# Windowed attention and a channel mix on one core: new engine choices, new orders, keys of the sinks copied on three engines

## The chip, the cores and the metric

The kernel runs on one core of one Trainium2 chip. The metric is the device time of one execution in microseconds. The five engines of the core work side by side and each takes its instructions in the order in which they were written: TensorE (PE; its weight loads are listed as PEld), VectorE (DVE), ScalarE (ACT), GpSimd (POOL) and SyncE (SP), which here only starts DMAs. Engines wait for one another through semaphores.

## The reference

Four batches of eight heads with 768 positions of 64 numbers go through attention with a window of 128 positions and four positions at the start (the sinks) that every query sees. The result, 768 x 512 per batch, goes through a channel mix with gate.

```python
keep = is_sink | in_window              # pos < 4, or 0 <= query - key < 128
a = softmax(where(keep, q @ k.T / 8, -1e9))
x = concat_heads(a @ v)                 # (4, 768, 512)
xk = mu_k * x + (1 - mu_k) * x_prev     # x_prev: one position earlier, zeros first
xr = mu_r * x + (1 - mu_r) * x_prev
k = maximum(xk @ w_k, 0)                # 512 -> 1024
v = (k * k) @ w_v                       # 1024 -> 512
out = sigmoid(xr @ w_r) * v
```

## The kernel before

The work is cut into 12 units u of 256 positions, three to a batch (T = 0, 1, 2). For each unit there are these steps:

- Load q, k and v of all heads in float32 (L479 to L509, on SP), and cast them to bf16 in halves (L732 to L743 for q and k, L813 for v). Then q and k are turned: for units 0 to 4 (k) and 0 to 6 (q) by PE and a copy out of PSUM (L776, L781, L794, L799), later by a transposing DMA on SP (L758). The results are `kt` and `qt`.
- `attend`: scores by pairs of heads (L877) into the tiles `sc`, exponentials on ScalarE (`e`, L949), a mask multiplied in on VectorE (L963), products with v on PE (L982), and division by the sums on VectorE (`rec`, L996; `x`, L999). In units 1 and 2 (the list `BIAS`) the mask is added on PE ahead of the scores (L886). In T = 1 and 2 the four sinks are a product of their own: their keys are copied out of `kt` into `ksink` (L830), scored with q of one or two units (L846), go through the exponential (`es`) and are multiplied with the sinks' values (`vsink`; L935 by quarters of the array, L920 in full form).
- `mix`: x is turned (by PE up to unit 5, L1023 and L1032; from unit 6 on by a transposing DMA, L1043, on SP), then `td`, `xk` and `xr` are made on VectorE (L1059, L1072).
- `ffn`: hidden products (L1150), relu (`rl`, L1160 or L1164), square (`kk`, L1172), gate (L1181, `th`), output products (L1199), result (`ob`, L1208), store (L1215, on SP).

The weights w_k, w_r and w_v come in 1 MB pieces (L522) and are cast by L693 to L699. PE's matmuls on the tile `warm` (L1257 to L1263) only fill gaps up to 28.5 us.

Every operation is recorded as one step of a `Plan` with a number (in the order of recording), a cost, the buffers that it takes and holds, and the data that it reads and writes. Two tables of numbers then settle the program. `CHOICE` names the engine, or the form on PE, for operations that can go several ways. `ORDER` gives, for each engine, the numbers in the order of issue. `schedule` walks these five lines, by its costs, in order to interleave them, assign buffers and place the gap fillers; it does not reorder within an engine. `LOADS` gives ranks to the first loads; the order on SP is the table's.

Of the kernel before, what the change touches and what calls it, by code (L numbers as in the profile page):

```python
# [18 lines left out]
    81: "DVE", 83: "ACT", 88: "ACT", 89: "DVE", 90: "DVE", 91: "ACT", 92: "POOL",  # L19
    93: "ACT", 94: "ACT", 95: "DVE", 96: "ACT", 97: "DVE", 98: "ACT", 100: "DVE",  # L20
    101: "DVE", 103: "ACT", 104: "POOL", 106: "DVE", 107: "POOL", 109: "ACT", 110:
    "POOL", 111: "DVE", 135: "POOL", 137: "ACT", 138: "DVE", 140: "DVE", 141: "ACT",
    143: "ACT", 144: "ACT", 146: "ACT", 147: "ACT", 148: "DVE", 150: "DVE", 157:
    "DVE", 167: "PE/tiles", 178: "PE/tiles", 187: "POOL", 189: "ACT", 190: "ACT",
    192: "ACT", 193: "POOL", 195: "ACT", 196: "POOL", 198: "ACT", 199: "POOL", 200:
    "ACT", 202: "DVE", 209: "ACT", 217: "ACT", 221: "ACT", 225: "DVE", 229: "ACT",
    247: "PE/tiles", 258: "PE/tiles", 267: "POOL", 269: "ACT", 270: "POOL", 272:
    "ACT", 273: "POOL", 275: "DVE", 276: "ACT", 278: "ACT", 279: "ACT", 280: "DVE",
    283: "ACT", 290: "DVE", 298: "DVE", 302: "ACT", 306: "ACT", 310: "DVE", 346:
    "POOL", 348: "ACT", 349: "POOL", 351: "ACT", 352: "ACT", 354: "ACT", 355: "DVE",  # L30
    357: "ACT", 358: "ACT", 359: "POOL", 361: "DVE", 368: "ACT", 376: "ACT", 380:
    "ACT", 384: "ACT", 388: "ACT", 402: "DVE", 403: "POOL", 405: "ACT", 406: "POOL",
    408: "ACT", 410: "ACT", 411: "ACT", 412: "ACT", 416: "PE/tiles", 428:
    "PE/tiles", 440: "ACT", 447: "ACT", 455: "ACT", 459: "ACT", 463: "ACT", 467:
    "ACT", 482: "PE/tiles", 494: "PE/tiles", 505: "POOL", 506: "ACT", 508: "ACT",
    509: "POOL", 511: "POOL", 513: "ACT", 514: "POOL", 515: "ACT", 518: "ACT", 525:
    "ACT", 533: "ACT", 537: "ACT", 541: "ACT", 545: "ACT", 581: "POOL", 582: "POOL",
    583: "ACT", 585: "POOL", 587: "POOL", 588: "DVE", 603: "ACT", 607: "ACT", 611:
    "ACT", 615: "ACT", 629: "ACT", 630: "ACT", 631: "ACT", 633: "POOL", 635: "ACT",
    636: "POOL", 640: "PE/tiles", 652: "PE/tiles", 677: "ACT", 681: "ACT", 685:  # L40
    "ACT", 689: "ACT", 704: "PE/tiles", 716: "PE/tiles", 727: "POOL", 728: "POOL",
    729: "ACT", 731: "POOL", 733: "ACT", 734: "ACT", 750: "ACT", 754: "ACT", 758:
    "ACT", 762: "ACT", 798: "POOL", 799: "POOL", 800: "ACT", 802: "ACT", 804:
    "POOL", 805: "DVE", 820: "ACT", 824: "ACT", 828: "ACT", 832: "ACT", 846: "ACT",
    847: "POOL", 848: "ACT", 850: "POOL", 852: "ACT", 853: "POOL", 857: "PE/full",
    869: "PE/tiles", 894: "ACT", 898: "ACT", 902: "ACT", 906: "ACT", 921:
    "PE/tiles", 933: "PE/full", 958: "ACT", 962: "DVE", 966: "ACT", 970: "ACT", 986:
    "DVE", 990: "ACT", 994: "ACT", 998: "DVE",
# [336 lines left out]
def kernel(  # L385
# [14 lines left out]
    nc = tc.nc  # L400
# [4 lines left out]
    NS = 4  # L405
# [44 lines left out]
    def act(n):  # L450
        return 80.0 + 0.805 * n
# [869 lines left out]
```

## Time and profile before

| what | value |
|---|---|
| median of 3 runs | 163.8 us (163.5 to 166.03) |
| profiled execution, its own time | 165.17 us |
| its span | 163.5 us |
| granted TensorE clock | 1.0 |
| PE, VectorE, ScalarE, GpSimd busy | 155.4, 144.3, 115.4, 35.5 us |
| HBM read, written | 24.15, 6.29 MB |

Busy time counts an instruction from its start to its end. Matmuls overlap, so PE's busy time also holds the tail of each; an idle stretch of PE that the profile names is one in which no matmul was under way. The chain of work is followed back from the last instruction: at each step to what released it, or to the instruction before it on its engine.

### The profile page before, as it was taken

The numbers are of one execution on the slowest core, as the hardware profiler recorded it, in microseconds if no ns is written. First come the engines' busy times: TensorE is split into PE (matmuls) and PEld (weight loads), VectorE is DVE, ScalarE is ACT, GpSimd is POOL, SyncE is SP. The second block draws the span as 40 slices with busy tenths as digits, with TensorE's granted clock in tenths as the row PEclk, the third lists the DMA queues.
The fourth block names the chain that finished last, engine by engine and source line by source line (L and its number), as shares of the span: only waits on it lengthen the run. The fifth ranks groups of instructions, "written<-read, shape, count | busy, mean of one in ns | idle before, by whom it ended". The sixth has DMA issues, their size and how long they took to land.

```text
span 163.5 us, 4724 instructions
## 1 busy us (share of the span) xinstructions
PE 155.4 (95%) x1867; PEld 101.1 (62%) x1867; DVE 144.3 (88%) x378; ACT 115.4 (71%) x182; POOL 35.5 (22%) x71
## 2 busy tenths in 40 slices
PE   7888999899999999999998989999999999999992
PEld 3445557785487557677484548567466856574841
DVE  5268987999999999999999699999989999998852
ACT  3388989999979899899867856867269977042220
POOL 5943402250032152130232303030040110000000
PEclk9999999999999999999999999999999999999999
DMA  4888999999899999999999999899999973180133
GB/s 144 242 242 220 321 339 338 384 386 347 206 271 273 204 219 231 203 278 138 192 188 255 150 296 245 148 256 144 262 213 233 224 236 64 32 190 38 64 128 128
DMA packets 80361, 35.46 MB, mean 217 GB/s; under 512 B 69964, under 2 KB 72276, under 8 KB 80340
## 3 DMA queue, kind: packets, MB, share of 16 engines
q1 hardware_dynamic: 80180, 34.97, 97.2%
q8 instruction: 14, 0.23, 0.6%
q10 hardware_dynamic: 160, 0.20, 0.3%
q14 instruction: 7, 0.06, 0.1%
HBM read 24.15 MB, written 6.29 MB: 186 GB/s over the span
## 4 chain that ended last, share of the span: by engine, by line
PE 61%; DVE 14%; DMA 10%; SPq 9%; ACT 2%; issue 1%; DVEq 0%
PE bank L1199 20%; PE bank L1150 19%; PE bank L1181 10%; DMA w<-in_moe_w_k_dram 7%; PE bank L982 4%; SPq L496 4%; DVE e L963 3%; PE sc L877 3%; SPq L479 3%; DMA xt<-x 3%; DVE x L999 2%; DVE xr L1072 2%; DVE xk L1072 2%; PE bank L776 2%; DVE kk L1172 2%
## 5 line engine op out<-in xcount | busy, mean ns | idle before, releaser
L949 ACT ACTIVATE e<-sc 128x1024 bf16<-128x1024 f32 (+1 forms) x48 | 44.6, 958 | 6.2 <-PE sc L877 6.2
L1150 PE MATMUL bank<-xk,wk_sb 128*128 128x256 bf16 x384 | 47.0, 273 | 0.6 <-DVE wk_sb L699 0.6
L1199 PE MATMUL bank<-wv_h,kk 128*128 128x512 bf16 x184 | 44.0, 379 | 0.0
L1150 PEld LDWEIGHTS <-wk_sb 128*128 128x128 bf16 x384 | 36.3, 98 | 6.9 <-DVE wk_sb L699 0.8
L1160 ACT ACTIVATE rl<-bank 128x512 bf16<-128x512 f32 x42 | 24.7, 604 | 18.9 <-PE bank L1150 17.5
L1199 PEld LDWEIGHTS <-kk 128*128 128x128 bf16 x184 | 16.9, 98 | 17.8 <-issue 0.2
L963 DVE TENSOR_TENSOR e<-e,mask 128x1024 bf16<-128x1024 bf16 (+1 forms) x40 | 25.3, 652 | 0.4 <-ACT e L949 0.4
L1181 PE MATMUL bank<-wr_sb,xr 128*128 128x512 bf16 x96 | 23.7, 379 | 0.0
L1072 DVE SCALAR_TENSOR_TENSOR xk<-td,mu_all,xt 128x256 bf16<-128x256 bf16 x48 | 23.4, 517 | 0.0
L1072 DVE SCALAR_TENSOR_TENSOR xr<-td,mu_all,xt 128x256 bf16<-128x256 bf16 x48 | 22.3, 484 | 0.0
L1172 DVE TENSOR_TENSOR kk<-rl 128x512 bf16<-128x512 bf16 x48 | 19.9, 430 | 0.9 <-ACT rl L1160 0.8
L1187 ACT ACTIVATE th<-bank 128x512 f32<-128x512 f32 x24 | 13.8, 604 | 8.9 <-PE bank L1181 8.9
L999 DVE TENSOR_TENSOR x<-bank,rec 128x256 bf16<-128x256 f32 x48 | 19.3, 415 | 0.4
L1208 DVE SCALAR_TENSOR_TENSOR ob<-th,bank 128x512 f32<-128x512 f32 x23 | 15.3, 677 | 2.8 <-ACT th L1187 1.9
L982 PE MATMUL bank<-vb,e 128*128 128x65 bf16 x352 | 16.3, 194 | 0.2 <-DVE vb L813 0.2
L982 PEld LDWEIGHTS <-e 128*128 128x128 bf16 x352 | 13.7, 97 | 3.5 <-issue 0.3
L1181 PEld LDWEIGHTS <-xr 128*128 128x128 bf16 x96 | 8.9, 98 | 8.5
L813 POOL CAST vb<-vs 128x512 bf16<-128x512 f32 x8 | 6.8, 856 | 31.4 <-DMA vs<-in_v_dram 21.7
L877 PE MATMUL sc<-qt,kt 64*64 64x128 bf16 (+3 forms) x496 | 12.7, 226 | 0.1
L877 PEld LDWEIGHTS <-kt 64*64 64x64 bf16 (+1 forms) x496 | 8.9, 106 | 6.0 <-issue 4.9
L736 POOL CAST qb<-qs 128x512 bf16<-128x512 f32 x8 | 5.8, 720 | 27.7 <-issue 9.5
L1059 DVE TENSOR_TENSOR td<-xt 128x512 bf16<-128x512 bf16 x24 | 9.9, 419 | 1.5 <-DMA xt<-x 1.4
(94 smaller groups left out, 153.0 us busy)
## 6 DMA issues: line engine op xcount, KB each, us to landing
vs<-in_v_dram SPq DMA_DIRECT2D x24, 256.0 KB, 5.5
out_dram<-ob SPq DMA_DIRECT2D x23, 256.0 KB, 3.7
ks<-in_k_dram SPq DMA_DIRECT2D x16, 256.0 KB, 4.3
qs<-in_q_dram SPq DMA_DIRECT2D x12, 256.0 KB, 4.2
qs<-in_q_dram SPq DMA_DIRECT2D x6, 512.0 KB, 11.8
ks<-in_k_dram SPq DMA_DIRECT2D x4, 512.0 KB, 7.6
w<-in_moe_w_k_dram SPq DMA_DIRECT2D x2, 1024.0 KB
w<-in_moe_w_v_dram SPq DMA_DIRECT2D x2, 1024.0 KB, 12.3
```

The lines of the kernel that those rows point to most:

```text
L877: nc.tensor.matmul(out=sc[keys, a, o0 + f0 - q0:o0 + f1 - q0], lhsT=lhs[rows, keys], rhs=qs[rows, f0:f1], start=u not in BIAS, stop=True, ...
L949: nc.scalar.activation(out=buf[ek][:, :, lo:], in_=buf[sck][:, :, lo:], func=AF.Exp, scale=scale)
L963: nc.vector.tensor_tensor(out=at, in0=at, in1=m, op=ALU.mult)
L982: nc.tensor.matmul(out=o[:, g, a, :], lhsT=e[:, a, e0:e0 + 128], rhs=rhs, start=(T == 0 and i == 0), stop=(i == len(blocks) - 1), skip_gro ...
L999: P.op("DVE", dve(256), lambda ok=ok, rk=rk, c=c: nc.vector.tensor_tensor(out=buf["x", u][:, :, 128 * c:128 * c + 128].rearrange("p g (a d ...
L1072: nc.vector.scalar_tensor_tensor(out=buf[key][:, c, :], in0=buf[tk][:, i, :], scalar=mu[w][:, c:c + 1], in1=xt[:, c, t0 - 1:t0 + 255], op0 ...
L1150: nc.tensor.matmul(out=ps[:, i, :], lhsT=wk_sb[:, c, 128 * f:128 * f + 128], rhs=xk[:, c, :], start=(c == 0), stop=(c == NC - 1), skip_gro ...
L1160: nc.scalar.activation(out=buf[rk], in_=buf[psk].rearrange("p (i t) -> p i t", i=2), func=AF.Relu)
L1172: P.op("DVE", dve(512, 0.52), lambda f2=f2, rk=rk: nc.vector.tensor_tensor(out=buf["kk", u][:, 2 * f2:2 * f2 + 2, :], in0=buf[rk], in1=buf ...
L1181: nc.tensor.matmul(out=buf[psk], lhsT=buf["xr", u][:, c, 128 * g:128 * g + 128], rhs=wr_sb[:, c, :], start=(c == 0), stop=(c == NC - 1))
L1199: nc.tensor.matmul(out=buf[psk], rhs=wv_h[:, f, :], lhsT=buf["kk", u][:, f, 128 * g:128 * g + 128], start=(f == 0), stop=(f == NF - 1))
L1208: P.op("DVE", dve(512), lambda psk=psk, tk=tk, bk=bk: nc.vector.scalar_tensor_tensor(out=buf[bk], in0=buf[tk], scalar=1.0, in1=buf[psk], o ...
```

## The change

In a few words it was described as: both loads of w_k ahead of unit 2's q and k, with the masks of units 1 and 2 on TensorE; GpSimd charged in full, sinks' keys copied off GpSimd; all orders anew.

The numbers in both tables are new, for all five engines. One operation is added (the fill of constants is cut in two, so all later numbers are one higher), the planner's costs of GpSimd's operations are raised, and the copy of the sinks' keys can go to three engines. The kernel's arithmetic and its buffers are as before. The lists `LOADS` and `BIAS` are not touched.

```diff
 CHOICE = {
-    81: "DVE", 83: "ACT", 88: "ACT", 89: "DVE", 90: "DVE", 91: "ACT", 92: "POOL",
+    82: "POOL", 84: "ACT", 89: "DVE", 90: "ACT", 91: "ACT", 92: "DVE", 93: "POOL",
...
     "SP": (
-        1, 0, 2, 3, 80, 7, 6, 4, 5, 16, 10, 15, 11, 8, 17, 9, 18, 20, 19, 12, 23,
+        1, 81, 0, 3, 2, 7, 6, 4, 5, 15, 16, 10, 11, 8, 17, 9, 18, 20, 19, 12, 23,
...
     def fill():
-        for t, value in ((ones, 1.0), (spread, 0.0), (hmask, 1.0), (rows, 1.0)):
+        nc.vector.memset(ones, 1.0)
+
+    def fill_blank():
+        for t, value in ((spread, 0.0), (hmask, 1.0), (rows, 1.0)):
             nc.vector.memset(t, value)
...
-    const_op("DVE", 500.0, fill, ["ones0"], rank=-80)
-    const_op("DVE", 1600.0, fill_later, ["sinks0", "ones", "edges"], rank=-79)
+    const_op("DVE", 260.0, fill, ["ones0"], rank=-80)
+    const_op("DVE", 1050.0, fill_blank, ["blank"], rank=-80)
+    const_op("DVE", 900.0, fill_later, ["sinks0", "ones", "edges"], rank=-79)
...
-                           "POOL": (620.0, cast(nc.gpsimd.tensor_copy), True)},
+                           "POOL": (740.0, cast(nc.gpsimd.tensor_copy), True)},
...
-        def sink_keys():
-            kz = ksink[b % 2].rearrange("p (c w) -> p c w", w=32)
-            for a in range(2):
-                rows = slice(64 * a, 64 * a + 64)
-                nc.gpsimd.tensor_copy(out=kz[rows, :, 4 * a:4 * a + NS],
-                                      in_=buf["kt", u][rows, :, 0, 0:NS])
-
-        P.op("POOL", 500.0, sink_keys, rank + 4, hold=[("kt", u)], port=True,
+        def sink_keys(copy):
+            def emit():
+                kz = ksink[b % 2].rearrange("p (c w) -> p c w", w=32)
+                for a in range(2):
+                    rows = slice(64 * a, 64 * a + 64)
+                    copy(out=kz[rows, :, 4 * a:4 * a + NS], in_=buf["kt", u][rows, :, 0, 0:NS])
+            return emit
+
+        P.op("POOL", 800.0, sink_keys(nc.gpsimd.tensor_copy), rank + 4, hold=[("kt", u)], port=True,
+             alts={"POOL": (800.0, sink_keys(nc.gpsimd.tensor_copy), True),
+                   "ACT": (360.0, sink_keys(nc.scalar.copy), False),
+                   "DVE": (180.0, sink_keys(nc.vector.tensor_copy), True)},
              reads=["sinks0", ("kt", u, 0), ("kt", u, 1)], writes=[("ksink", b % 2)])
```

On PE all that is new in kind is one pair of sinks' products of unit 1 in full form. For the four casts of w_k, VectorE and ScalarE change places. Three places show what moved. Lines of the changed kernel stand up to nine higher from the added operations on.

**SP, from the second v of unit 0 to the first of w_r.** `qs2_72` and `ks2_69` take unit 2's q and k, `w320_76` and `w321_77` the halves of w_k, `vs1` and `vs2` v of units 1 and 2. Before:

```order
L496 DMA qs2_72<-in_q_dram 128x2x512
L479 DMA vs1_74<-in_v_dram 128x8x64
L496 DMA ks2_69<-in_k_dram 128x2x512
L479 DMA vs1_74<-in_v_dram 128x8x64
L522 DMA w320_76<-in_moe_w_k_dram 128x4x512
L479 DMA vs2_75<-in_v_dram 128x8x64
L522 DMA w321_77<-in_moe_w_k_dram 128x4x512
```

Now:

```order
L497 DMA ks2_69<-in_k_dram 128x2x512
L497 DMA qs2_72<-in_q_dram 128x2x512
L480 DMA vs1_74<-in_v_dram 128x8x64 x2
L523 DMA w320_76<-in_moe_w_k_dram 128x4x512
L480 DMA vs2_75<-in_v_dram 128x8x64
L523 DMA w321_77<-in_moe_w_k_dram 128x4x512
```

Unit 2's k and q change places and stand together; both loads of w_k keep their places, behind them. Earlier on SP, the load of the sinks' values moves from the fifth place to the second, ahead of k of unit 0.

**The copy of the sinks' keys of units 6 to 8.** It is the row with `ksink0_154<-kt2_87`. Before, on GpSimd, where `qb` and `kb` are casts of q and k, `vb` of v:

```order
L736 CAST qb2_84<-qs2_72 128x4x128
L813 CAST vb3_138<-vs1_74 128x8x64
L736 CAST qb0_82<-qs0_70 128x4x128
L830 COPY ksink0_154<-kt2_87 64x4x4 x2
L736 CAST qb0_82<-qs0_70 128x4x128
```

Now, on ScalarE (`rl` is relu, `th` the gate, `e` an exponential, `xt` a copy out of PSUM):

```order
L958 ACTIVATE e3_96<-sc0_61 128x2x384
L1196 ACTIVATE th1_129<-bank1_64 128x512
L741 CAST qb2_84<-qs2_72 128x4x128
L1169 ACTIVATE rl4_127<-bank0_63 128x512
L836 COPY ksink0_154<-kt2_87 64x4x4 x2
L1041 COPY xt1_161<-bank1_64 128x2x256
L1169 ACTIVATE rl3_126<-bank0_63 128x512
```

The copy leaves the engine where the cast of unit 9's first q stood ahead of it; ahead of it now are the cast of unit 8's second q and a relu. On PE, the scores of units 7 and 8 with these keys stood behind the second half of unit 7's window scores; now they stand ahead of those, of three groups of four hidden products of unit 5 and of one group of products with v.

**VectorE around unit 6's first `td`.** The `td` rows are the first that read x of unit 6 after its transposing DMA (`xt0_160`); `x1_108` is unit 7's x. Before:

```order
L999 TENSOR_TENSOR x1_108<-bank3_66,rec4_105 128x2x128
L1172 TENSOR_TENSOR kk2_122<-rl3_126 128x512
L1172 TENSOR_TENSOR kk2_122<-rl4_127 128x512
L1059 TENSOR_TENSOR td1_111<-xt0_160 128x512
L999 TENSOR_TENSOR x1_108<-bank0_63,rec5_106 128x2x128
L1059 TENSOR_TENSOR td2_112<-xt0_160 128x512
```

Now:

```order
L1008 TENSOR_TENSOR x1_108<-bank1_64,rec0_101 128x2x128
L1181 TENSOR_TENSOR kk2_122<-rl4_127 128x512
L1008 TENSOR_TENSOR x1_108<-bank2_65,rec4_105 128x2x128
L1068 TENSOR_TENSOR td1_111<-xt0_160 128x512
L1068 TENSOR_TENSOR td0_110<-xt0_160 128x512
```

Unit 7's second x stood behind the first `td` and now stands ahead of it; it frees a bank of PSUM that the next sinks' products on PE take. On PE, an output product of unit 5 (eight matmuls of L1199) moves ahead of these sinks' products, and one of unit 4 with a pair of unit 8's scores behind them.

More of the change, by code (lines that the diff above doesn't have):

```diff
@@ L25 @@
[L25 to L48, printed above, removed]
+    82: "POOL", 84: "ACT", 89: "DVE", 90: "ACT", 91: "ACT", 92: "DVE", 93: "POOL",
+    94: "ACT", 95: "DVE", 96: "DVE", 97: "ACT", 98: "DVE", 99: "DVE", 101: "DVE",
+    102: "ACT", 104: "ACT", 105: "DVE", 107: "DVE", 108: "ACT", 110: "DVE", 111:
@@ new lines @@
+    "ACT", 112: "DVE", 113: "DVE", 136: "DVE", 138: "ACT", 139: "POOL", 141: "DVE",
+    142: "POOL", 144: "ACT", 145: "ACT", 147: "ACT", 148: "POOL", 149: "DVE", 151:
+    "DVE", 158: "DVE", 168: "PE/tiles", 179: "PE/full", 188: "POOL", 190: "ACT",
+    191: "POOL", 193: "ACT", 194: "ACT", 196: "ACT", 197: "POOL", 199: "ACT", 200:
+    "POOL", 201: "DVE", 203: "DVE", 210: "ACT", 218: "ACT", 222: "ACT", 226: "ACT",
+    230: "ACT", 248: "PE/tiles", 259: "PE/tiles", 268: "DVE", 270: "ACT", 271:
@@ new lines @@
+    "PE/tiles", 678: "ACT", 682: "ACT", 686: "ACT", 690: "ACT", 705: "PE/tiles",
+    717: "PE/tiles", 728: "ACT", 729: "POOL", 730: "ACT", 732: "ACT", 734: "ACT",
+    735: "POOL", 736: "ACT", 751: "ACT", 755: "ACT", 759: "ACT", 763: "ACT", 799:
+    "POOL", 800: "ACT", 801: "POOL", 803: "ACT", 805: "POOL", 806: "DVE", 821:
+    "ACT", 825: "ACT", 829: "ACT", 833: "ACT", 847: "DVE", 848: "DVE", 849: "ACT",
+    851: "ACT", 853: "POOL", 854: "POOL", 858: "PE/full", 870: "PE/tiles", 895:
+    "ACT", 899: "ACT", 903: "ACT", 907: "ACT", 922: "PE/tiles", 934: "PE/full", 959:
@@ L49 @@
+    "ACT", 963: "ACT", 967: "ACT", 971: "ACT", 987: "DVE", 991: "ACT", 995: "ACT",
+    999: "ACT",
 }
```

40 lines of the change are left out of this document (24 added, 16 removed), and 136 rows, old and new, of the table ORDER.

## The prediction

> **What bounds the kernel now.** I read the page's busy shares first, then the same by stage, then the chain, and then the waits of TensorE (PE) inside the stage that differs. The stages (columns: stretch; busy us of PE, PE's weight loads, VectorE, ScalarE, GpSimd; granted clock; DMA share; GB/s):
>
> ```profile
> 0.00:29.20 29.20, 25.50 (x323) 15.19 (x323) 20.20 (x64) 21.69 (x34) 12.44 (x37) 1.00 0.92 266
> 29.20:60.00 30.80, 30.78 (x380) 20.85 (x383) 30.16 (x75) 28.45 (x46) 8.15 (x13) 1.00 1.07 288
> 60.00:80.00 20.00, 19.95 (x285) 14.20 (x278) 19.93 (x52) 18.49 (x32) 4.98 (x7) 1.00 1.29 214
> 80.00:95.00 15.00, 13.88 (x226) 8.83 (x225) 13.49 (x36) 10.96 (x17) 3.91 (x6) 1.00 1.30 200
> 95.00:160.00 65.00, 65.00 (x675) 41.93 (x672) 59.87 (x154) 35.85 (x57) 6.06 (x9) 1.00 0.83 170
> ```
>
> From 29.2 on PE has next to no visible idle time: 0.02, 0.05, 1.12 and 0.00 us, together 1.19 us. VectorE is as full up to 80 us (30.16 of 30.8, 19.93 of 20), ScalarE is at 28.45 of 30.8 and 18.49 of 20, and GpSimd alone has room. What sets 29.2 is a transfer; the chain of work that ended last says which (start, length, what):
>
> ```profile
> 16.85 11.60 DMA w<-in_moe_w_k_dram
> 28.47 0.70 DVE wk_sb L699
> 29.22 1.92 PE bank L1150 x16
> ...
> 89.34 4.34 DMA xt<-x
> ...
> 151.56 3.49 PE bank L1150 x32
> ```
>
> So there are three parts: until 28.47 the second half of w_k is on its way; then PE, VectorE and ScalarE run nearly full together; from 94.6 the chain is PE alone. Both visible PE waits after 29.2 stand in the timeline, with what ended them:
>
> ```profile
> 87.01 0.40 PE L846 MATMUL bank<-qt,ksink 128*32 128x256 bf16 x8 [0.49 <-POOL ksink L830]
> 94.59 0.30 PE L935 MATMUL bank<-vsink,es 64*64 64x130 bf16 x6 [0.63 <-DVE x L999]
> ```
>
> These 0.49 and 0.63 us are the 1.12 us. A new order of the same work can take from PE after 29.2 about these 1.2 us; more has to come from before 29.2, or from matmuls that start a little apart, which the busy time does not show.
>
> **The change part by part.** *The w_k loads.* The first one's issue in SyncE's (SP's) queue (the second's is the chain's 16.85), and the wait for the second:
>
> ```profile
> 14.45 1.79 SPq L522 DMA_DIRECT2D w<-in_moe_w_k_dram  x1
> 28.47 0.69 DVE L699 CAST wk_sb<-w 128x1024 bf16<-128x1024 f32 x1 [0.97 <-DMA w<-in_moe_w_k_dram]
> ```
>
> In SP's rows above, q and k of unit 2 stand ahead of both loads of w_k before and after; only their own order is swapped. The bytes ahead are the same, so I take the landing at 28.47 unchanged: 0 us. Nor does the set of PE operations ahead of the first product that needs the second half of w_k change. Against that, the sinks' loads move up ahead of k of unit 0:
>
> ```profile
> 2.96 1.29 SPq L660 DMA_DIRECT2D vs<-in_v_dram  x2
> 4.64 0.62 ACT L741 CAST kb<-ks 128x512 bf16<-128x512 f32 x1 [1.48 <-DMA ks<-in_k_dram]
> 5.32 0.38 PE L781 MATMUL bank<-ident,qb 128*128 128x128 bf16 x4 [0.42 <-POOL ident L593]
> 9.89 1.02 DVE L963 TENSOR_TENSOR e<-e,mask 128x768 bf16<-128x768 bf16 x2
> 12.76 0.61 POOL L732 CAST kb<-ks 128x512 bf16<-128x512 f32 x1 [1.80 <-DMA ks<-in_k_dram]
> 15.78 0.39 DVE L999 TENSOR_TENSOR x<-bank,rec 128x256 bf16<-128x256 f32 x1
> ```
>
> That is 1.29 us later for k, partly paid back by the identity matrix, now first on GpSimd (0.42 us of wait goes), and by the VectorE cast, 0.2 us shorter than ScalarE's 0.62. VectorE now also casts unit 1's first k (landed only at 12.76), queued ahead of unit 0's masks; behind it wait three masks (0.51 us each by the row at 9.89), a copy, a cast, a product and small operations (0.4 to 0.7 each), about 4 us in all, and then unit 0's first x (15.78 before). From 12.7 on this gives 16.7, 0.9 us late. The cover is the 0.97 us in which VectorE waited for w_k: cost 0, or 0.9 us if that cover is gone. From -0.4 (an earlier start) to +0.9, I take 0, nearest to the row with 0.97.
>
> *Sinks' keys off GpSimd.* On GpSimd they stood behind a cast that waited for its DMA:
>
> ```profile
> 85.27 0.86 POOL L736 CAST qb<-qs 128x512 bf16<-128x512 f32 x1 [2.72 <-DMA qs<-in_q_dram]
> 86.08 0.88 POOL L830 COPY ksink<-kt 64x16 bf16<-64x16 bf16 x2
> ```
>
> For units 6 to 8 and 9 to 11 they go to ScalarE, for 0 to 2 to VectorE, for 3 to 5 they stay. No row has this copy on ScalarE; the nearest there is a small cast:
>
> ```profile
> L676 ACT CAST rows<-bank 128x256 bf16<-128x256 f32 x1 | 0.4, 375 | 0.0
> ```
>
> Two copies of a sixteenth of its columns take from next to nothing to 0.75 us; I take 0.5, near the row, and it lies in ScalarE's load below. The wait of 0.49 us goes. What is late next is q of unit 8, which the same scores read:
>
> ```profile
> 80.12 2.11 SPq L758 DMA_TRANSPOSE qt<-qb  x1
> 85.99 0.53 PE L877 MATMUL sc<-qt,kt 64*64 64x192 bf16 x24
> ```
>
> The list of DMA issues has, with the median us to landing at the end:
>
> ```profile
> kt<-kb SPq DMA_TRANSPOSE x7, 3.6
> qt<-qb SPq DMA_TRANSPOSE x5, 5.0
> ```
>
> Without the wait PE would have come to the sinks' scores at 86.5, behind the row at 85.99. Now these scores (0.5 us), 12 matmuls of L1150 (0.109 each by the chain's 3.49 us for 32: 1.3 us) and six small ones (0.2) stand behind them, so PE comes 2.0 us earlier, at 84.5. Transposes land 3.6 us (kt) to 5.0 us (qt) after issue, so this one at 83.7 to 85.1: a new wait of 0 to 0.6 us. Net -0.5 to +0.1; I take -0.3.
>
> *Unit 6's x transposes.* In the timeline of SP, VectorE and PE:
>
> ```profile
> 86.92 0.58 SPq L489 DMA_DIRECT2D ks<-in_k_dram  x1
> 87.59 3.01 SPq L1043 DMA_TRANSPOSE xt<-x  x2
> 93.77 0.43 DVE L1059 TENSOR_TENSOR td<-xt 128x512 bf16<-128x512 bf16 x1 [1.40 <-DMA xt<-x]
> 95.18 0.68 DVE L963 TENSOR_TENSOR e<-e,mask 128x1024 bf16<-128x1024 bf16 x1
> 97.07 0.45 DVE L1072 SCALAR_TENSOR_TENSOR xk<-td,mu_all,xt 128x256 bf16<-128x256 bf16 x1
> 97.91 1.36 PE L1150 MATMUL bank<-xk,wk_sb 128*128 128x256 bf16 x11
> ```
>
> Unit 7's second x now goes ahead of the `td` that waits 1.40 us for xt, and PE has an output product of unit 5 ahead of the sinks' products that wanted this x; so their wait of 0.63 us goes. The transposes themselves start no earlier: SP reaches them after the same count of issues, without a pause (the issue at 86.92 ends at 87.50). What is late next is unit 6's xk, done at 97.52, for a PE that came at 97.91: 0.39 us of room. Between the wait and this xk a mask (0.68) and an x (0.39 by the row at 15.78) leave VectorE and an xr (0.45, like the xk) comes: 0.6 us more. Hence PE can gain 1.0 us by here, and -0.3 from the sinks and -0.6 from here fit. This term alone lies between -0.63 and, if xk comes late after all, 0.
>
> *Casts redistributed.* GpSimd goes from 46 planned operations to 40, ScalarE gets 6 more, VectorE none on balance. At ScalarE's 0.62 us a cast (row at 4.64) that is 3.7 us at most over the span; three of the six, 1.9 us, fall between 60 and 95 (the casts of units 6 to 9 and a copy of keys). ScalarE's idle time there is 1.51 us (60 to 80) and 4.04 (80 to 95). Cover for most; xt of unit 5, on ScalarE, is the first that VectorE would wait for. 0 to +1.9; I take +0.3, near the full cover. After 95 ScalarE is at 35.85 of 65 and the two relus that move from VectorE cost nothing. Fewer casts on GpSimd could shorten VectorE's; I take 0, as VectorE runs into the same xt at 93.77 anyway. The rest of the orders and the split memsets: 0, from -0.5 to +0.5, as PE's work is the same but for one product in full form (0.11 us, ahead of the gate).
>
> Sum: 0 - 0.3 - 0.6 + 0.3 = **-0.6 us**. The profiled execution took 165.17 us (span 163.5 and 1.67 around it): 164.6. It lies 1.37 us over the median of 163.8, so the same shift on the median gives 163.2.
>
> **The rivals.** *ScalarE becomes the bound (slower).* If the 1.9 us of new casts find only the 1.51 us of idle time to 80 us, and that idle time is itself waiting for PE's products, exponentials come up to 1.9 us late, masks and values behind them, and PE with no other work: 163.8 + 1.9 = 165.7, less up to 0.9 if the two waits still go. It decides once ScalarE is over 1.5 us behind at 80 us. For it: 92% busy; against: the products were reordered with it.
>
> *GpSimd's casts held VectorE, and fewer free it.* The rows bear it out:
>
> ```profile
> 19.13 1.40 POOL L732 CAST kb<-ks 128x512 bf16<-128x512 f32 x2 [2.25 <-DMA ks<-in_k_dram]
> 19.22 0.83 DVE L1072 SCALAR_TENSOR_TENSOR xk<-td,mu_all,xt 128x256 bf16<-128x256 bf16 x1
> 20.73 0.47 DVE L1072 SCALAR_TENSOR_TENSOR xk<-td,mu_all,xt 128x256 bf16<-128x256 bf16 x1
> ```
>
> The same operation took 0.83 us beside a cast and 0.47 alone: 0.36 us each. Six casts fewer give up to 2.2 us, and if half of it is on the path, 163.2 - 1.1 = 162.1. Against it stands the xt transfer. The Trainium skill (SBUF — State Buffer, Who interferes with whom) states that a VectorE instruction with two SBUF inputs contends with a GpSimd instruction that reads SBUF; the trace agrees with its 0.83 against 0.47. The same place says that ScalarE never waits for another engine there, which speaks for the casts' new home, and no row here speaks against it.
>
> *The change does not do what its words say.* They speak of w_k ahead of unit 2's q and k. If it landed ahead of them (1 MB at the 266 GB/s of the first stage, 3.9 us), the gate would move to some 25 us and the time to near 160. The order excludes it: 0.03.
>
> **How the numbers follow.** Forecast (162.4 to 164.4): 0.52. ScalarE or another new wait: 0.25, of which 0.10 over 167.1 us, where it comes about twice. VectorE freed: 0.20 (to 161.3). Earlier gate or all gaps closed: 0.03. Taking the two outer cases by their bounds, 161.4 to 166.2 leaves out 2 in 10. A measurement of this kernel tells 2%, 3.3 us, from no change (three runs lay 2.5 us apart): faster than 160.5 0.04, slower than 167.1 0.10, within 0.86.
>
> **What would show it.** w_k's cast near 28.5 and PE's gate near 29.2 (first term). No PE wait released by a sinks' copy, at most 0.6 us by q's transposes (second). No wait at L944's products, td still waiting for xt near 93 (third). ScalarE's lead at 60 to 80 us: xt of unit 5 not named as what VectorE waits for (fourth). A new PE wait of over 1 us in 30 to 80 us, a gate that moved by a microsecond, or SP late with a transpose would make it wrong.

## The result and the profile after

The changed kernel takes 165.2 us in the median of 18 executions (163.51 to 167.21), the kernel before 163.8 us in 18 beside them (162.74 to 166.31). The ratio is 1.0072, with a 95% interval of 1.0048 to 1.0095: slower by 0.7%, 1.2 us by the ratio and 1.4 between the two medians, where 0.6 us faster was forecast. Ratios here leave out executions over 1.5% above a kernel's own fastest; the changed kernel has many of these (11 of 28, before 13 of 104), so medians of all are given too: 165.5 us over its 28 executions in this study, 164.2 over 104 of before.

Yet the profiled execution of the changed kernel was faster than that of before: 164.46 against 165.17 us, span 162.7 against 163.5. Read alone it looks like the forecast come true. The stages (columns as in the prediction):

```profile
0.00:29.20 29.20, 25.03 (x328) 15.77 (x329) 22.31 (x70) 22.56 (x35) 11.26 (x35) 1.00 0.98 284
29.20:60.00 30.80, 29.96 (x376) 19.85 (x374) 30.61 (x70) 27.50 (x47) 10.40 (x14) 1.00 1.04 276
60.00:80.00 20.00, 19.65 (x265) 13.71 (x262) 19.93 (x51) 18.57 (x33) 3.60 (x6) 1.00 1.09 210
80.00:95.00 15.00, 15.00 (x242) 9.72 (x240) 14.75 (x42) 13.26 (x20) 1.39 (x2) 1.00 1.01 221
95.00:160.00 65.00, 64.32 (x656) 41.21 (x654) 59.23 (x151) 35.58 (x59) 4.19 (x6) 1.00 0.82 167
```

PE's 1.12 us of idle time at 80 to 95 us are gone, and VectorE is at 30.61 of 30.8 between 29.2 and 60. What is left of PE's waits behind 28 us, in the timeline of PE of the changed kernel (start, length, what, and in brackets the idle time and what ended it):

```profile
35.91 0.30 PE L944 MATMUL bank<-vsink,es 64*64 64x130 bf16 x6 [0.70 <-DVE xt L1041]
60.99 1.03 PE L1159 MATMUL bank<-xk,wk_sb 128*128 128x256 bf16 x8 [0.17 <-DVE ob L1217]
63.34 0.31 PE L944 MATMUL bank<-vsink,es 64*64 64x130 bf16 x8 [0.18 <-DVE x L1008]
113.94 0.35 PE L991 MATMUL bank<-vb,e 128*128 128x65 bf16 x6 [0.16 <-ACT rl L1169]
```

The sinks' copy and the x of unit 7 release no wait any more; a new one of 0.70 us stands at 35.9. On VectorE the second half of w_k is cast at 26.53 instead of 28.47 us, and nothing is waited for there:

```profile
26.53 0.69 DVE L704 CAST wk_sb<-w 128x1024 bf16<-128x1024 f32 x1
```

So one profile says -0.7 us and 18 executions say +1.2. The two profiled executions lie at different places of their distributions: that of before 1.4 us above its median, that of the changed kernel 0.8 below. More traces of both kernels were needed first of all.

### The profile page after: what moved, and what is told of

Read it like the earlier page. It is cut to its first block, busy times and chain, and to the rows that moved or that the text cites. A ratio compares the mean times of both kernels' runs of the same rounds, so it can differ in the third digit from the quotient of the medians.

```text
span 162.7 us, 4709 instructions
## 1 busy us (share of the span) xinstructions
PE 154.0 (95%) x1856; PEld 100.3 (62%) x1856; DVE 146.8 (90%) x379; ACT 117.5 (72%) x190; POOL 30.8 (19%) x62
## 4 chain that ended last, share of the span: by engine, by line
PE 58%; DVE 27%; DMA 8%; issue 2%; SPq 2%; ACT 0%; DVEq 0%; ACTq 0%
PE bank L1208 18%; PE bank L1159 14%; PE bank L1190 10%; PE bank L991 5%; DVE xk L1081 4%; DVE xr L1081 4%; PE sc L886 4%; DVE e L972 4%; DMA qs<-in_q_dram 3%; DMA ks<-in_k_dram 3%; DVE x L1008 3%; DMA xt<-x 2%; DVE kk L1181 2%; DVE td L1068 1%; DVE ob L1217 1%
## 5 line engine op out<-in xcount | busy, mean ns | idle before, releaser
L1159 PE MATMUL bank<-xk,wk_sb 128*128 128x256 bf16 x384 | 47.7, 273 | 0.2 <-DVE ob L1217 0.2
L958 ACT ACTIVATE e<-sc 128x1024 bf16<-128x1024 f32 (+1 forms) x48 | 44.1, 958 | 4.8 <-PE sc L886 3.8
L1169 ACT ACTIVATE rl<-bank 128x512 bf16<-128x512 f32 x46 | 27.1, 603 | 18.0 <-PE bank L1159 16.7
L1208 PEld LDWEIGHTS <-kk 128*128 128x128 bf16 x184 | 17.0, 98 | 17.5 <-DVE kk L1181 0.4
L1081 DVE SCALAR_TENSOR_TENSOR xr<-td,mu_all,xt 128x256 bf16<-128x256 bf16 x48 | 24.3, 518 | 0.0
L1181 DVE TENSOR_TENSOR kk<-rl 128x512 bf16<-128x512 bf16 x48 | 20.5, 443 | 1.6 <-ACT rl L1169 1.5
L1196 ACT ACTIVATE th<-bank 128x512 f32<-128x512 f32 x24 | 14.4, 606 | 8.2 <-PE bank L1190 7.8
L818 POOL CAST vb<-vs 128x512 bf16<-128x512 f32 x12 | 8.8, 736 | 37.5 <-DMA vs<-in_v_dram 35.3
L991 PEld LDWEIGHTS <-e 128*128 128x128 bf16 x352 | 13.5, 97 | 3.9 <-issue 0.6
L886 PE MATMUL sc<-qt,kt 64*64 64x128 bf16 (+4 forms) x496 | 12.6, 226 | 0.5 <-DVE sc L591 0.5
L737 POOL CAST qb<-qs 128x512 bf16<-128x512 f32 x8 | 6.2, 782 | 20.9 <-DMA qs<-in_q_dram 16.8
```

The lines of the kernel that those rows point to most:

```text
L886: nc.tensor.matmul(out=sc[keys, a, o0 + f0 - q0:o0 + f1 - q0], lhsT=lhs[rows, keys], rhs=qs[rows, f0:f1], start=u not in BIAS, stop=True, ...
L958: nc.scalar.activation(out=buf[ek][:, :, lo:], in_=buf[sck][:, :, lo:], func=AF.Exp, scale=scale)
L991: nc.tensor.matmul(out=o[:, g, a, :], lhsT=e[:, a, e0:e0 + 128], rhs=rhs, start=(T == 0 and i == 0), stop=(i == len(blocks) - 1), skip_gro ...
L1081: nc.vector.scalar_tensor_tensor(out=buf[key][:, c, :], in0=buf[tk][:, i, :], scalar=mu[w][:, c:c + 1], in1=xt[:, c, t0 - 1:t0 + 255], op0 ...
L1159: nc.tensor.matmul(out=ps[:, i, :], lhsT=wk_sb[:, c, 128 * f:128 * f + 128], rhs=xk[:, c, :], start=(c == 0), stop=(c == NC - 1), skip_gro ...
L1169: nc.scalar.activation(out=buf[rk], in_=buf[psk].rearrange("p (i t) -> p i t", i=2), func=AF.Relu)
```

## The experiments

**More traces.** e5, e6 and e16 are the two kernels, unchanged.

> The kernel before, unchanged, for a second trace of it. Theory 'loads': the profiled execution of before (165.17 us) was one in which the first loads moved slowly (250 to 300 GB/s from 8 to 11 us) and SyncE's tenth issue was held until 12.50 us; an execution near the median of 163.8 us shows a higher rate and that issue near 11.5 us, and the rest of the span as before. Rival 'late part': the same start, and the time won behind 60 us.

> The changed kernel, unchanged, for a second trace. Theory 'loads': its profiled execution (164.46 us, below its median of 165.2) had the early loads at 370 GB/s and SyncE's tenth issue (unit 2's q) at 11.09 us; a typical one has that issue nearer to 13.1 us, as e2 with the same start, unit 1's q cast at 12 instead of 10 us, and TensorE later by 1 to 2.5 us from there to the end. Rival 'late part': the start as in the first trace, and the time lost behind 60 us.

> The kernel before, unchanged, for a third trace, since both so far (165.17 and 164.60 us) lie above its median of 164.0 us. Theory 'gate': in an execution at or under the median the two halves of w_k land sooner than 28.3 us and TensorE's gate moves with them, one for one to the end. Rival 'middle': the gate stays, and the time comes out of the waits at 87 and 95 us.

Measured: before 164.60 us (e5) and 164.25 (e16); the changed kernel 167.60 us in its trace (e6), median of ten executions 166.1 against 163.9 for before beside them (the ratio, 1.0001 with 0.9939 to 1.0062, rests on three of the ten and decides nothing). This table is worked out from the traces; "k lands" is the last completion record of unit 1's k, "scores" the start of unit 1's first scores on PE, "gate" that of the first hidden product that needs the second half of w_k, "hidden" that of unit 2's first hidden product, "rest" the time from there to the start of the last output product.

| trace | k lands | scores | between | gate | hidden | rest | own time |
|---|---|---|---|---|---|---|---|
| before | 12.63 | 15.69 | 3.06 | 29.22 | 45.52 | 114.36 | 165.17 |
| e5, before | 12.40 | 15.68 | 3.28 | 29.08 | 45.34 | 113.95 | 164.60 |
| e16, before | 11.94 | 15.22 | 3.28 | 27.81 | 44.15 | 114.80 | 164.25 |
| after | 11.36 | 15.62 | 4.26 | 27.52 | 44.78 | 114.38 | 164.46 |
| e6, after | 13.36 | 18.51 | 5.15 | 30.78 | 47.69 | 114.62 | 167.60 |

Three things follow. In these five traces the rest is the same within the spread. And from the landing of k to unit 1's scores the changed kernel needs 4.3 to 5.2 us where before needs 3.1 to 3.3. In its first trace that was hidden, since k landed 1.3 us sooner than in the trace of before. e6 lost 2.9 us by the scores and 3.15 at the end: between these two, what the start lost reached the end whole.

The third lies between the gate and unit 2's hidden products: 16.3 us in each of the three traces of before, 17.3 and 16.9 in the two of the changed kernel. The changed kernel's wait of PE at 35.9 us is there again in e6:

```profile
38.82 0.30 PE L944 MATMUL bank<-vsink,es 64*64 64x130 bf16 x6 [0.48 <-DVE xt L1041]
```

Of the thirteen traces in this study with the new rows at that place, eleven have this wait (0.42 to 0.72 us) and take 16.9 to 17.5 us from gate to unit 2; e4 and e8 are without it and take 16.5. None of the seven traces with the old rows has it: five of these take 16.2 to 16.3 us, and e14 and e15, which wait there for something else, 16.8 and 17.2. So the changed kernel loses 0.6 to 1.0 us here in both of its traces, and no run takes that away. Ahead of the gate it wins time: 11.9 and 12.3 us from scores to gate, without a wait of PE for w_k, against 12.6 to 13.5.

The expectation 'loads' was right for e6 (SyncE's tenth issue at 13.17 us) and only half right for e5 and e16, whose tenth issues came at 12.24 and 11.7: in e16 the gate moved as 'gate' says (1.4 us earlier), but 'middle' is seen as well. The timeline of PE in e5 has these waits behind 28 us:

```profile
48.74 0.40 PE L776 MATMUL bank<-ident,qb 128*128 128x128 bf16 x4 [0.20 <-DVE qb L732]
62.00 0.38 PE L776 MATMUL bank<-ident,qb 128*128 128x128 bf16 x4 [0.29 <-DVE ob L1208]
119.38 0.81 PE L1199 MATMUL bank<-wv_h,kk 128*128 128x512 bf16 x3 [0.16 <-issue]
```

and in e16 these:

```profile
47.52 0.40 PE L776 MATMUL bank<-ident,qb 128*128 128x128 bf16 x4 [0.19 <-DVE qb L732]
82.63 0.60 PE L1150 MATMUL bank<-xk,wk_sb 128*128 128x256 bf16 x4 [0.22 <-DVE ob L1208]
112.52 0.35 PE L982 MATMUL bank<-vb,e 128*128 128x65 bf16 x6 [0.88 <-ACT rl L1160]
119.03 0.81 PE L1199 MATMUL bank<-wv_h,kk 128*128 128x512 bf16 x3 [0.16 <-issue]
```

Neither has the wait at L846 nor that at L935, on which the prediction rested two of its terms.

How e6 loses its start is in its timeline of VectorE:

```profile
11.28 0.53 DVE L972 TENSOR_TENSOR e<-e,mask 128x768 bf16<-128x768 bf16 x1
13.38 0.43 DVE L737 CAST kb<-ks 128x512 bf16<-128x512 f32 x1 [1.56 <-DMA ks<-in_k_dram]
13.72 0.76 DVE L836 COPY ksink<-kt 64x16 bf16<-64x16 bf16 x2
14.52 0.17 DVE L658 COPY mu_all<-bank 128x8 f32<-128x8 f32 x1
14.60 0.68 DVE L799 COPY qt<-bank 128x512 bf16<-128x512 bf16 x1
15.31 1.03 DVE L972 TENSOR_TENSOR e<-e,mask 128x768 bf16<-128x768 bf16 x2
```

VectorE stands still for 1.56 us ahead of the cast of unit 1's k. Of unit 0's four masks, of which before makes two at 9.89 us, e6 makes one at 11.28 and the next two only at 15.31. The first trace of the changed kernel shows the same row without the wait:

```profile
10.24 0.19 DVE L585 MEMSET ksink<- 128x64 uint32 x2
...
10.79 0.31 DVE L591 MEMSET sc<- 64x128 f32 x2
11.01 0.53 DVE L972 TENSOR_TENSOR e<-e,mask 128x768 bf16<-128x768 bf16 x1
11.47 0.41 DVE L737 CAST kb<-ks 128x512 bf16<-128x512 f32 x1
...
13.38 1.03 DVE L972 TENSOR_TENSOR e<-e,mask 128x768 bf16<-128x768 bf16 x2
```

Meanwhile PE has little to do, and its granted clock falls; the stages of e6 (columns as before, the clock ahead of the last two):

```profile
8.00:10.00 2.00, 0.71 (x9) 0.49 (x6) 1.13 (x3) 1.51 (x2) 0.00 (x0) 1.00 0.89 297
10.00:12.00 2.00, 1.38 (x11) 0.36 (x9) 1.79 (x12) 0.14 (x1) 0.11 (x1) 1.00 1.15 301
12.00:14.00 2.00, 1.02 (x12) 0.72 (x13) 0.62 (x2) 1.89 (x3) 1.09 (x2) 1.00 0.41 88
14.00:16.00 2.00, 1.31 (x14) 0.81 (x13) 1.92 (x6) 1.46 (x4) 0.28 (x1) 0.89 0.89 248
16.00:18.00 2.00, 2.00 (x20) 1.25 (x19) 1.14 (x3) 1.52 (x4) 1.07 (x3) 0.50 1.09 356
18.00:20.00 2.00, 1.96 (x45) 1.64 (x43) 1.98 (x9) 0.91 (x1) 1.73 (x4) 0.76 1.31 251
```

At 0.50 PE gets less done in the same busy time: the four matmuls of L895 that take 1.03 us in the first trace of the changed kernel, at 13.52, take 1.81 in e6, at 15.45. The half clock lasts about 3.4 us in e6; this is an estimate from the three rows under 1.00, taking the clock as either 1.00 or 0.50 (0.44, 2.0 and 0.96 us). It can cost at most half of that, 1.7 us. Of the 28 executions of the changed kernel 8 have a mean clock of 0.990 or less, of the 104 of before none. Those eight average 166.9 us, the other twenty 165.0, before 164.3: of the 1.2 us between the means, 0.6 belong to the executions in which the clock fell. These eight are 2.0 us behind the twenty, more than the fall itself can cost by the estimate, so they are late for another reason as well.

**Old and new tables, mixed.** All of e1 to e4 have the changed code.

```diff
 # e1: the tables of before (numbers from 72 on one higher)
-ORDER, CHOICE = those of after
+ORDER, CHOICE = those of before
 # e2 (e3): after where the plan starts before (behind) 60 us, else before
 # e4: the first 12 of SyncE as before
-        1, 81, 0, 3, 2, 7, 6, 4, 5, 15, 16, 10,
+        1, 0, 2, 3, 81, 7, 6, 4, 5, 16, 10, 15,
```

> The changed code (split memset, the three engines that may copy the sinks' keys, the new prices) with the old tables: the sinks' keys are copied by GpSimd, and every engine has the order of before; only the fill products at the start and the choice of buffers may differ. Theory 'orders': the +0.7% over the runs comes from the new tables, so this one takes 1.000 of the time before, within 0.002. Rival 'code': the new memsets, buffers or fills cost it, and this one takes 1.005 to 1.009.

> The changed code; instructions planned before 60 us stand on the engines and in the orders of after, those behind it as before. Theory 'first stage': VectorE, which in the trace of after runs without a gap from 24.4 to 49.4 us, passes what it loses there to the end, so this one takes 1.005 to 1.009 of the time before. Rival 'later': ScalarE's added operations and the new order of DMAs behind 60 us cost the time, and this one takes 0.995 to 1.001.

> The complement: instructions planned before 60 us as before, those behind it as after. Theory 'first stage': 0.996 to 1.001 of the time before (the trace of after reaches the hidden products of unit 6 1.4 us early, by the order behind 60 us). Rival 'later': 1.005 to 1.009.

> The changed kernel with the first 12 DMA issues of SyncE in the order of before (both halves of unit 0's k and q ahead of the sinks' loads; unit 2's k behind the first half of w_k as before). Theory 'start': the sinks' loads ahead of k delay the first cast by 1.6 us (k landed at 6.26 instead of 4.64 us in the two traces), part of which reaches the end, so this one takes 1.000 to 1.004 of the time before. Rival: the start is made up for by the wait for w_k or by VectorE's unbroken row of work, and this one stays at 1.005 to 1.009.

Measured: e1 1.0073 (1.0027 to 1.0119), e2 1.0203 (1.0150 to 1.0257), e3 1.0125 (1.0062 to 1.0188), e4 1.0284 (1.0221 to 1.0347). The halves do not add up, and every mixture is slower than the whole, so e2 and e3 decide nothing about the place: the likely reason, not shown, is that a seam has its own price, as a planner's buffers and fill products change with every table. e4 misses both of its ranges and does not test its theory alone, as it moves unit 2's k too: with that load two issues later, GpSimd's cast of it starts at 18.5 us instead of 14.8, and in the new row of GpSimd a mask and two more casts stand behind it.

e1 is the surprise: old orders with the new prices lose as much as the change. Since the orders are equal, buffers and fill products are left, beside the finer wait that the split memset allows.

**Which of the two e1 pays for.** e15 is the kernel before, with e1's fill products in the place of its own; e12 is the reverse of e1, the new orders with the old prices.

```diff
 # e15, kernel before: 18 fill products (35 units of width) for 16 (26)
-        for i in self.schedule():
+        order = [i for i in self.schedule() if not isinstance(i, tuple)]
+        # ... e1's fills put ahead of the same PE operations, in banks free there
+        for i in order:
```

> The kernel before, its orders and buffers as they are, with the fill products of e1 (18 with 35 units of width, four of them 128x512 in FP32 twice over right behind unit 0's first scores) in the place of its own 16 with 26. Theory 'fills': these delay unit 0's second half by 1.1 us (its transposed k at 10.31 instead of 9.18 us in e1), and that is the loss of e1: 1.004 to 1.009. Rival 'buffers': 0.998 to 1.002, and e1's loss comes from the buffers that the new prices choose.

> The reverse of e1: the orders and engines of after with the prices of before, so that all five engines' orders are those of after and only the buffers chosen and the fill products differ (23 units of width instead of 21). Theory 'start': the row of VectorE and the loads are those of after, so 1.005 to 1.010. Rival 'buffers': the new prices picked worse buffers (e1 lost 0.7% with the old orders), so 0.998 to 1.002.

Measured: e15 1.0121 (1.0065 to 1.0176); e12 1.0153 (1.0103 to 1.0203). 'Fills' is right in kind for e15, though its loss lies above the range, and 'buffers' is wrong: the fill products alone cost about 1% (0.7 to 1.8). e12, too, lies above both of its ranges. The timeline of PE in e15 shows where:

```profile
8.01 0.50 PE L909 MATMUL sc<-qt,kt 64*128 64x256 bf16 x8
8.44 1.98 PE L1295 MATMUL bank<-warm 128*128 128x512 f32 x4
10.27 0.39 PE L813 MATMUL bank<-ident,kb 128*128 128x128 bf16 x4
```

Two microseconds of fill hold the second half of unit 0's k, which stood at 8.75 us in before. Unit 1's scores follow 4.19 us behind the landing of k, hidden products of unit 2 begin at 46.40, and the rest takes 113.75 us. Nothing but the start was touched, and 1.2% was lost at the end: this is the clearest evidence that a loss at the start reaches the end. (e1, with the same fill products, has its scores 3.53 us behind the landing in its one trace; its median of 12 is 165.8 us, and its trace at 164.41 one of the faster ones.) e12 has a start as in after (scores 4.28 us behind the landing) and loses more later, by a wait that the next experiment is about.

**A late transposition.** In the traces of e6, e7, e8 and e12 PE waits at unit 9's first scores; the timelines of PE in e6 and in e12:

```profile
102.89 0.52 PE L886 MATMUL sc<-qt,kt 64*64 64x256 bf16 x16 [0.86 <-DMA kt<-kb]
```

```profile
102.54 0.52 PE L886 MATMUL sc<-qt,kt 64*64 64x256 bf16 x16 [2.22 <-DMA kt<-kb]
```

The change brings PE there 1.5 us sooner (100.12 instead of 101.63 in the two first traces), the transposition on SyncE only 0.5. e13 issues it earlier:

```diff
     # SyncE's row near 92 us: store of unit 4 (555), v of unit 8 (48), kt of unit 9 (731)
-    555, 733, 48, 731,
+    733, 731, 48, 555,
```

> The changed kernel with one change in SyncE's row near 92 us: the transposition of unit 9's k goes ahead of the store of unit 4's output and of the second load of unit 8's v, which now follow it. Theory 'late transposition': in the traces e6, e7, e8 and e12 TensorE waits 0.86 to 2.22 us at unit 9's first scores for that transposition, which after the change has 1 us less cover; issued 0.6 to 1.5 us sooner it no longer ends that wait, the trace shows no wait there, and the time comes to 1.001 to 1.005 of before. Rival 'start': it stays at 1.006 to 1.009.

Measured: 1.0117 (1.0062 to 1.0172). The wait is gone, and the time is not better; in its place PE waits 0.60 us for an x at 107.2. The theory falls as the cause. That such waits come and go is seen in "rest": 113.75 to 114.80 us in six traces with the old rows behind 60 us (mean 114.2), 114.01 to 116.32 in eleven with the new (mean 115.0); e2 to e4 with their seams or moved loads are left out (115.8, 114.7, 115.4). The two of the changed kernel itself lie at 114.5, but seven of the others differ from it at the start alone. So a loss of up to 0.8 us behind unit 2's hidden products is possible beside that of the start, and is not shown.

**The start, edit by edit.** e7, e9 and e17 change only where an instruction stands, e8 adds fill products (four, with widths 4, 1, 2 and 1), and e10, e11 and e18 do both; the plan's buffers are kept. e14 makes the edit of e7 the other way round in the kernel before.

```diff
+        order.remove(81)                          # e7: sinks' loads fifth
+        order.insert(order.index(2) + 1, 81)
+MORE = ((140, 4), (140, 1), (137, 2), (143, 1))   # e8: fills (ahead of, width)
+        for i in (116, 113):                      # e9: unit 0's mask and sinks' keys
+            order.remove(i)                       #     ahead of unit 1's cast (136)
+            order.insert(order.index(136), i)
+        order.remove(72)                          # e17: memsets first
+        order.insert(order.index(71) + 1, 72)
 # e10: e7 and e9, with MORE = ((140, 1), (137, 1), (143, 1), (83, 1), (128, 1))
 # e11: e10 without e9. e18: e10 with e17. e14: sinks' loads second, in before
```

> The changed kernel, with every engine's order, buffer and fill product as they are, but the two loads of the sinks' values issued fifth on SyncE, behind the four of unit 0's k and q, as before the change; unit 2's k stays the first of unit 2's loads. Theory 'sinks ahead': the small packets (27 GB/s around 3.5 us) put off the whole row of loads by about 1 us, which reaches the end: 1.000 to 1.003 of the time before. Rival 'fills': it stays at 1.006 to 1.009.

> The changed kernel with five more fill products (widths 4, 1, 2 and 1) ahead of unit 1's transposes of q and k, between 10 and 14 us, and nothing else changed. Theory 'clock': where unit 1's q lands late, TensorE is idle for over half of 10 to 14 us and its granted clock falls to 0.50 (in the trace of e2, 16 to 18 us); more fills take that away, so the runs' granted clock no longer falls to 0.99 and the time comes to 1.001 to 1.005 of before. Theory 'loads' alone: no change of the median (1.006 to 1.009), since the landing sets the start.

> The changed kernel with two moves in VectorE's row alone: the mask of unit 0's first scores and the copy of unit 0's sinks' keys stand ahead of the cast of unit 1's k, instead of behind it; everything else as it is. Theory 'row': where k of unit 1 lands late, VectorE stands still for 1.6 us ahead of that cast with 1.3 us of work for unit 0 queued behind it; with that work in the gap the late executions come 1 us earlier, so the median falls to 1.001 to 1.004 of before, and in the trace unit 1's first scores stand at 16.5 to 17.5 us where q lands near 12 us. Rival 'clock': the fall of TensorE's clock behind its idle time sets the start, and the median stays at 1.006 to 1.010.

> The changed kernel with three edits at the start: VectorE's row as in e9, the sinks' loads fifth as in e7, and five fill products of 128x512 between 10 and 15 us (ahead of unit 1's transposes, of the product that spreads the sinks' values and of unit 0's first output). Theory 'start': every cause named lies there, so the loss goes and what the change wins behind 60 us remains: 0.993 to 1.001 of before, clock 0.995 or more in every run. Rival 'later': 1.004 to 1.008.

> As e10 without the edit of VectorE's row. Theory 'clock and landing': 0.997 to 1.003, no clock under 0.995. Theory 'row': 1.003 to 1.007, since the work of unit 0 still waits behind the cast of unit 1's k.

> The kernel before with one edit: the sinks' loads stand second on SyncE instead of fifth, as the change has them. Theory 'loads': k of unit 1 then lands either near 11.4 or near 13.3 us (the traces of after and its kin), where it lands at 12.1 to 12.6 us with the loads fifth, and the spread of the runs grows; 1.003 to 1.008. Rival: the old row of VectorE, which casts unit 1's k on GpSimd and has unit 0's masks ahead, does not feel it: 0.998 to 1.002.

> The changed kernel with one move in VectorE's row: the ten memsets (sinks' keys, borders, the zeros beside unit 0's scores) go back ahead of unit 0's casts, where the kernel before has them (2.3 us) and VectorE waits for k of unit 0 anyway; the change has them at 10.2 to 11.1 us, ahead of unit 0's masks and the cast of unit 1's k, and unit 0's second scores wait 0.55 us for the last of them. Theory 'VectorE's row at the start': 0.5 to 0.9 us at that place, most of it to the end: 1.000 to 1.004 of before. Rival 'landing': where k of unit 1 lands late, the memsets lie in VectorE's wait for it and their move wins nothing: 1.006 to 1.010.

> All edits of the start together: the memsets first (e17), unit 0's mask and sinks' keys ahead of unit 1's cast (e9), the sinks' loads fifth (e7) and five narrow fill products (e11). Theory 'start': 0.994 to 1.001. Rival 'what is left is not the start' (e10 without the memsets' move took 1.007): 1.004 to 1.008.

| run | ratio to before | interval | executions, of them with clock 0.990 or less | k lands to scores |
|---|---|---|---|---|
| changed kernel | 1.0072 | 1.0048 to 1.0095 | 28, 8 | 4.26, 5.15 |
| e7 sinks fifth | 1.0065 | 1.0025 to 1.0106 | 12, 7 | 4.94 |
| e8 wide fills | 1.0112 | 1.0058 to 1.0167 | 6, 0 | 5.42 |
| e9 VectorE's row | 1.0044 | 0.9993 to 1.0096 | 12, 3 | 4.61 |
| e10 = e7, e9, narrow fills | 1.0067 | 1.0027 to 1.0107 | 12, 2 | 4.80 |
| e11 = e7, narrow fills | 1.0057 | 1.0014 to 1.0100 | 12, 0 | 4.21 |
| e17 memsets first | 1.0112 | 1.0055 to 1.0169 | 6, 1 | 4.14 |
| e18 = e10, memsets first | 1.0031 | 0.9995 to 1.0067 | 12, 0 | 3.51 |
| e14, before, sinks second | 0.9996 | 0.9962 to 1.0031 | 12, 0 | 3.70 |

No single edit is shown to give the loss back. The theories of e7, e8, e10, e14 and e17 are missed; e11 fits its theory 'row', and e9 and e18 fall between their two ranges. Over all their executions e9 stands at 165.85 us against 164.27 of before beside it, and e18 at 164.96 against 164.46; e9's ratio rests on six of its twelve. The sinks' loads are not it from either side (e7, e14). Fill products keep the clock up (e8, e11), and the time does not follow. So the fall of the clock seems to go with the late start rather than to make it, unless the fills cost what the clock gives back; that is not separated. All edits together come to 1.0031, with scores 3.51 us behind the landing, near the 3.1 to 3.3 of before; their interval takes in 1.000 and reaches into that of the changed kernel, so that they give back about half of the loss is likely and not shown. VectorE's timeline in e18 shows the row that they aim at:

```profile
9.38 1.10 DVE L1005 TENSOR_TENSOR e<-e,mask 128x768 bf16<-128x768 bf16 x2
10.39 0.34 DVE L869 COPY ksink<-kt 64x16 bf16<-64x16 bf16 x2
12.41 0.43 DVE L770 CAST kb<-ks 128x512 bf16<-128x512 f32 x1 [1.67 <-DMA ks<-in_k_dram]
12.75 0.16 DVE L691 COPY mu_all<-bank 128x8 f32<-128x8 f32 x1
```

Two of unit 0's masks and its keys stand ahead of the wait now, not behind it. No version of the changed kernel beats before.

Two parts of the change none of these runs puts back. One is the wait of PE near 36 us: 0.71 us in e18. The other is PE's own row at the start. In the timeline of PE, before has 18 of unit 0's 24 products with v ahead of unit 1's first scores and six behind them:

```profile
14.97 0.80 PE L982 MATMUL bank<-vb,e 128*128 128x65 bf16 x18
15.69 0.53 PE L877 MATMUL sc<-qt,kt 64*64 64x192 bf16 x24
16.16 0.35 PE L982 MATMUL bank<-vb,e 128*128 128x65 bf16 x6
```

The changed kernel has all 24 ahead:

```profile
14.47 1.22 PE L991 MATMUL bank<-vb,e 128*128 128x65 bf16 x24
15.62 0.53 PE L886 MATMUL sc<-qt,kt 64*64 64x192 bf16 x24
```

So up to 0.4 us of the later scores can lie in this order and not in VectorE's row; e18 keeps it (24 in 0.95 us).

## Why the prediction was wrong, step by step

**The start and the w_k gate (0 us, from -0.4 to +0.9): the step that failed.** The prediction saw the row: unit 1's k cast by VectorE ahead of unit 0's masks, some 4 us of work behind it, 0.9 us late. It then set the cost to nothing for the 0.97 us in which VectorE waited for w_k. That cover belongs to one execution of before: in e5 VectorE waits 0.61 us at that cast, in e16 not at all, as there the loads were quicker. Nor is the lateness fixed at 0.9. Unit 0's first x, which stood at 15.78 us and was put at 16.7, comes at 16.12 in the first trace and at 18.78 in e6: 4.65 and 5.40 us behind the start of the cast of k, where the sum took about 4. Scores come 4.3 to 5.2 us behind the landing of k instead of 3.1 to 3.3, so 1 to 2 us, and in about three of ten executions the clock falls on top. The end of the range that was not taken was nearer the truth. Not all of this is VectorE's row, since PE's order ahead of these scores changed as well. "The landing unchanged" did not hold in either direction: the first issue of w_k stood at 13.02 us in the first trace and at 15.10 in e6, against 14.45.

**The rest of the orders (0, from -0.5 to +0.5): a second step that failed.** "PE's work is the same" was the reason for this 0, and a wait is not work: PE's new wait for VectorE's xt near 36 us makes the stretch from the gate to unit 2's hidden products 0.6 to 1.0 us longer in both traces of the changed kernel. The prediction looked for new waits of PE at the places that it went through one by one, and this one was not among them.

**Sinks' keys (-0.3) and unit 6's transposes (-0.6): right in what goes, wrong in what it is worth.** Both waits are gone in the trace after, with none by q's transposes in their place, as foretold. But of three traces of before only the first has them; of the wait at L935, e15 has 0.93 us once more. A wait seen in one execution was booked as a property of the kernel. From unit 2's hidden products to the end the changed kernel takes 114.38 and 114.62 us, before 113.95 to 114.80: the two terms and ScalarE's +0.3 together were -0.6 us, and measured is +0.1 (means of two and three traces, 114.50 and 114.37), with a spread of 0.85 among the three. VectorE waits for unit 6's xt only in e6 (0.81 us), not in the first trace, which meets "still waiting near 93" by half.

**ScalarE (+0.3).** No wait of VectorE for ScalarE's xt appeared, and the two copies of keys that were estimated at 0.5 us take 0.4 there, 0.20 each; the groups of the changed kernel by the tile `ksink`:

```profile
L836 ACT COPY ksink<-kt x4: 190/200/205, 78.4 to 109.5; 64x16 bf16<-64x16 bf16 x4
L836 DVE COPY ksink<-kt x2: 170/372/575, 11.8 to 12.4; 64x16 bf16<-64x16 bf16 x2
L836 POOL COPY ksink<-kt x2: 343/360/378, 48.1 to 48.5; 64x16 bf16<-64x16 bf16 x2
```

**The rivals.** ScalarE as the bound is refuted by the absence of its wait. VectorE freed by GpSimd is not seen: the blend `xk` takes 514 ns on the mean after and 517 before, `xr` 518 and 484. The words of the change (w_k ahead of unit 2's q and k) do not describe its order, as the prediction said. What came is "another new wait", which it had inside its range and with a chance of 0.25: one at a place that it had named and priced, one near 36 us that it had not. Of its own marks, "a gate that moved by a microsecond" was met: 27.52 in the first trace and 30.78 in e6, against 29.22. So was "SP late with a transpose", in e6 (0.86 us at 102.89).

**The baseline.** The sum was made against an execution 1.4 us above the median and then moved to the median as it stood. That is sound only if what makes such an execution slower does not touch the terms. Here the late loads that made it slow gave it the cover, and the waits that were to be won were its own too.

What stays open: which share of the loss lies in VectorE's row, in PE's row at the start, in the clock, in the wait near 36 us and in the waits behind 60 us, and why unit 1's k lands anywhere from 11.2 to 13.4 us with the sinks' loads second (11.17, 11.36, 11.44, 11.82, 12.71, 12.81, 13.32, 13.36 us in eight traces of the new tables, 11.70 in e14).

## What to carry to other kernels

Before a wait of half a microsecond is booked as a gain, or an idle half microsecond as cover, look whether it stands in a second and a third trace of the same program. Here PE's two waits of before stood in neither of two more traces, while the new wait near 36 us came back in eleven of thirteen. On an engine that takes its work in order, no instruction that waits for a load whose landing varies should stand ahead of work that is ready: the row then has the spread of the load. And when prices in a planner change, the buffers and gap fillers that it picks change with them, which alone cost 0.7 to 1.2% here with every order kept.

## What the runs showed of the hardware

- The granted clock of TensorE fell to 0.50 between 16 and 18 us after 3.1 us of work in the 6 us from 8 to 14 (e6); with 4.25 us of work in them it stayed at 1.00 (e8). In e7 it fell sooner, to 0.58 between 12 and 14 us, after 2.70 us of work in the 4 us from 8 to 12, where e8 had 2.25 and did not fall; so such a sum alone does not draw the line. Nor was PE ever idle for long: its longest waits between 8 and 16 us of e6, in its timeline of PE, are

```profile
9.35 0.40 PE L786 MATMUL bank<-ident,kb 128*128 128x128 bf16 x4 [1.29 <-DVE kb L746]
...
12.56 0.40 PE L781 MATMUL bank<-ident,qb 128*128 128x128 bf16 x4 [0.63 <-POOL qb L737]
```

  The Trainium skill (TensorE: Matmul & The Clock Gate, "HAM oscillation — how this bites in real kernels") warns of idle gaps longer than about 3.4 us. The half clock that it names agrees with 0.50 here; the gap does not, since no idle stretch of PE in e6 between 8 us and the fall was longer than 1.29 us.
- The same first loads, in the same order, land up to 2.2 us apart (unit 1's k: 11.17 to 13.36 us). With them moves the issue of unit 2's q on SyncE, which stands behind the longest hold of the start: 11.09 and 13.17 us in the two traces of the changed kernel.
- Two copies of 64x16 numbers on VectorE took 0.76 us beside a GpSimd cast and 0.34 without (e6 and e18, rows above), more than twice as long.
